# One core, linear-memory attention and MLP: first loads on two queues, segment 0 in token halves, its blocks in borrowed space, a new order of work

## The chip, the cores and the metric

One core of a Trainium2 chip runs the kernel. The metric is device time in microseconds. The kernel before has a median of 305.55 us over three runs (305.26 to 305.59). The profile and its trace are of one separate execution, whose span from the first to the last instruction is 303.6 us.

## The reference

One pre-norm transformer block over 2048 tokens of width 640: attention with 32 heads of 20, in 4 segments of 512 tokens with a running memory, and then an MLP of width 1728.

```python
h  = x + A(layernorm(x))          # A: attention below, wq wk wv wo of 640x640
h2 = h + silu(layernorm(h) @ w1) @ w2

# A, for each segment s of 512 tokens, M and z start at 0
p     = softmax(q_s k_s^T * 20**-0.5 + causal mask)
a_dot = p @ v_s
a_mem = (phi(q_s) @ M) / (phi(q_s) @ z + 1e-6)
o_s   = sigmoid(beta) * a_mem + (1 - sigmoid(beta)) * a_dot
M, z  = M + phi(k_s)^T v_s, z + sum(phi(k_s))
# phi(t) = t + 1 where t > 0, else exp(t); the output is o @ wo
```

Inputs, weights and output are bf16; sums are kept in f32.

## The kernel before, in words

The program is a list of some 1,500 small tasks written out by hand in `ORDER` (L358 to L457). `Graph.schedule` (L287) reads it: each entry names a task, its engine where it has a choice (`/A` ACT, `/D` DVE, `/G` POOL) and the buffer slots it takes. Each engine gets its own tasks in the order of the list and works them off in that order. `Tracker.add` (L79) finds out which earlier task wrote or still reads what a task touches, and puts a wait in front of it. A waiting task holds up everything behind it on its engine. DMA starts are instructions of such a queue too: nearly all stand on SP, two on ACT.

The steps of a segment s (of four blocks of 128 tokens) and their names:

- `x0` to `x3`, `x4`, `x8`, `x12` load x (`load_x`, L564): one block each for the first four, four blocks at a time for the others. `w_wv`, `w_q`, `w_k` load the attention weights; wq and wk land in the space of `sT` and are copied into groups of four heads by `re_wq0` to `re_wk4` (L663).
- `n1_stB`, `n1_raB`, `n1_rbB`, `n1_apB` are the layer norm of block B (L701): statistics on DVE, variance + eps and the power -0.5 on POOL, then the scaling on DVE. For blocks 0 to 3 PE transposes the result (`n1_tpB`) and ACT or DVE copies it out of PSUM (`n1_teB`); the later ones are transposed by a DMA (`n1_trB`).
- `vSI` and `veSI` are the V projection of a block and its way out of PSUM (L783, L794). `prSCW` projects head group C, for Q (W = 0) or K (W = 1), over all 512 tokens in five matmuls (L817), and `qeSCW` casts it to bf16 (L826 on DVE, L825 on ACT). PSUM has eight banks of 512 f32 columns, and the list says which one a task takes.
- Heads have 20 rows of 32, so the remaining 12 rows hold parts of heads 20 to 31; 12 small DMAs per segment (`vt`, L857) put these together in `QKV`, for the head groups (ticks) 5 to 7.
- A tick is one group of four heads: `qk` scores in four row tiles (L893), `e` exponentials on ACT (L904), `mk` causal masks on POOL (L915), `av` the product with V in four column tiles (L936), `oe` out of PSUM, `tn` back to token order, `nm` the division. In segment 0 each tick is worked in two halves of the tokens: `x` for the first 256 and `y` for the last.
- `ex`, `pha`, `phb` make phi; `kt`, `mz`, `ma`, `mb` the memory; `ot`, `wo`, `rs` the output projection and the residual; `n2_` the second layer norm, transposed into `hT`; `h1`, `th`, `s` the first MLP product and its activation (L1153, L1162, L1168); `h2`, `o`, `out` the second product, the residual and the store (L1195, L1208, L1213). The last 64 of the 1728 hidden columns (`h1_S_13`) are done in two column tiles of 64 (L1148).
- `fillN` are N matmuls on zeros (L604) that compute nothing.

In segment 0 `wq`, `wk` and `wv` come in the order wv, wq, wk, behind x1 and x0 on SP, with x3 and x2 on ACT. `w1` is loaded in five pieces and `w2` in six, at various places of SP's queue.

Of the kernel before, what the change touches and what calls it, by code (L numbers as in the profile page):

```python
# [5 lines left out]
ACT = mybir.ActivationFunctionType  # L6
ALU = mybir.AluOpType
# [340 lines left out]
SPLIT0 = ()  # L348
# [10 lines left out]
zpad:0 vpad0 iota x3:4 x1:3 x0:7 x2:5 sel w_wv:0 warm:0 vpad1 w_q:0 w_k halfc epsc beta x4:0,1,2,6 n1_st0:1 w_wo:0  # L359
w_w2_4 n1_st1:6 n1_ra0 w_w1_0:0 n1_rb0 n1_ap0:0 n1_ra1 n1_st2:2 fill30:0 n1_tp0:4 n1_rb1 n1_te0/A:0 n1_st3:0 n1_ra2  # L360
epsg0 n1_rb2 fill8:1 v00:0 mt1 n1_ap2:1 n1_ra3 n1_ap1:0 n1_rb3 n1_tp1:2 n1_tp2:6 mt2 n1_ap3:2 n1_te1/A re_wq1/D:0
n1_tp3:4 n1_te2/A re_wq4/D v01:2 ve00/D:1 n1_te3/A re_wq2/A pr010:6 re_wk0/A:0 re_wk1/D ve01/D pr011:7 qe010/D:0
re_wk3/D re_wk4/A lsc0 lsc1 re_wq0/D pr001:0 re_wk2/D qe011/A qk1x0:4 qe001/D:0 pr000:1 e1x2:5 n1_st6:0 e1x0 pr021:0
re_wq3/D qe000/A n1_ra6 mk1x_0 lsc2 n1_st7:4 ex001:0 qk0x0:4 n1_rb6 pr020:2 e0x2:0 mt3 mk1x_256 qe021/D:0 e0x0 lsc3
pr041:3 n1_st5:5 qe020/A vt00:0 n1_st4:7 qk2x0:4 n1_ra5 qe041/A:0 mk0x_0 pr031:1 zf0 vt09 vt06 e2x2:2 n1_rb5 mk0x_256
pr030:0 e2x0 n1_ap5:2 pha041:1 x8:8,9,10,11 qe031/A:0 mk2x_0 vt03 qk0yb0:4 qe030/D av1x:3 e0yb0:1 pr040:2 mk2x_256
n1_ra7 pha001:0 e0yb2 oe1x/D:0 av0x:3 qe040/D mk0yb_0 qk1yb0:4 oe0x/A:1 av2x:0 e1yb0:3 tn1x:1 v03:2 pha021:2 nm1x:3,0
e1yb2 mk0yb_256 phb001 n1_ap6:1 oe2x/A:0 mk1yb_0 qk3x0:4 ve03/D v02:0 n1_tr5:0 vt011 vt07 e3x2:4 vt04 n1_rb7 n1_st9:1
e3x0 ex021:2 ve02/D vt05 vt010 qk4x0:4 mk3x_0 n1_ra4 tn0x:2 e4x0:6 nm0x:0 vt01 mk3x_256 e4x2 n1_st8:6 fill7:3 qk0ya0:0
mta1 vt02 av3x:4 e0ya0:5 mk4x_0 vt08 oe3x/D:1 n1_st10:0 mk4x_256 e0ya2 fill6:5 qk1ya0:4 n1_tr6 v11:0 n1_rb4 e1ya0:0  # L370
n1_st11:3 n1_ra10 mta3 kt00:1 n1_ra8 e1ya2 av4x:2 ve11/D:0 tn2x:3 n1_ra11 phb021 qk5x0:4 n1_ap4:3 fill10:0 v12:0 e5x2:2
n1_ap7:1 n1_tr4 oe4x/D:0 e5x0 nm2x:1 ex011:2 n1_tr7 ve12/D qk6x0:4 mk5x_0 tn4x:2 e6x0:4 av0y:3 nm4x:0 mk5x_256 tn3x:0
e6x2 oe0y/D:0 kt02:0 n1_rb11 av5x:1 ex041:1 n1_ap11:3 qk7x0:4 mk6x_0 v10:2 nm3x:1 w_w2_5 e7x2:6 oe5x/D:1 mta2 mtb3 e7x0
mk6x_256 w_w1_1 w_w1_4 ve10/D qk2ya0:4 mk7x_0 v13:0 e2ya2:5 n1_ra9 mk7x_256 mk1yb_256 e2ya0 tn0y:2 av7x:3 ve13/D n1_rb8
oe7x/A:0 qk2yb0:4 nm0y:1 tn7x:0 e2yb0:1 av6x:1 nm7x:2 tn5x:2 av1y:3 e2yb2 oe6x/D:1 nm5x:3 tn6x:0 oe1y/A:0 qk3ya0:4
# [24 lines left out]
mk12e_0 qk13b0:4 qe231/D:0 tn11:2 e13b2:5 pr200:0 mk12e_256 nm11:3,0 ad10 e13b0 av12:1 qe200/D:0 mk13b_0 qk14a0:4 v23:2  # L400
e14a2:1 phb140 mk13b_384 oe12/D:1 mb04:0 e14a0 av13:1 ve23/A qk14b0:4 mz13:0 e14b2:3 pr221:2 ma13 oe13/D:0 e14b0
h1_0_7_1:3 qe221/A mk14b_0 qk14e0:4 th0_7_1:1 tn13:0 s0_7_1 mk14a_0 pr211:2 nm13:3,1 mk14b_384 e14e0:0 e14e2 h1_0_8_1:3
qe211/D mk14e_0 qk15a0:4 th0_8_1:1 pr241:0 e15a0:4 s0_8_1 mk14e_256 ad11 e15a2 av14:2 qe241/D:0 ad13 mz11:1 oe14/A:0
# [57 lines left out]
def build(nc, es, A_x, A_wq, A_wk, A_wv, A_wo, A_beta, B_x, B_w1, B_w2, out):  # L461
# [229 lines left out]
    for c in range(NC):  # L691
        load_w(f"w1_{c}", w1_sb[:, c, :], B_w1[128 * c:128 * c + 128, :], -1 + 0.2 * c, 1.4, [(W["w1"], [c])])
# [576 lines left out]
```

## Time and profile before

| | us |
|---|---|
| runs, median of 3 | 305.55 |
| span of the profiled execution | 303.6 |
| first filler on PE | 1.12 |
| first matmul of the computation (transposition of block 0) | 7.36 |
| first scores | 16.33 |
| first exponential | 16.72 |
| last matmuls begin | 289.81 (97 of L1195, 11.48) |

The costliest groups of instructions by engine:

| line | engine, what | count | busy us | mean ns |
|---|---|---|---|---|
| L904 | ACT, exponentials | 168 | 156.3 | 985 |
| L915 | POOL, masks | 128 | 81.5 | 650 |
| L1195 | PE, second MLP product | 462 | 64.8 | 295 |
| L1153 | PE, first MLP product | 325 | 62.5 | 337 |
| L1168 | DVE, activation | 70 | 37.6 | 558 |
| L604 | PE, fillers | 61 | 9.1 | 310 |

Busy time of PE counts each matmul from its start to its modelled end; dense matmuls start closer together than that. The fillers stand in it as busy. PEclk, the granted clock, is 1.00 in every window.

### The profile page before, as it was taken

The page shows a single profiled execution, that of the slowest core. Times are in us where ns is not written, and L with a number is a line of the kernel's source. Part 1 is how long each engine was busy: PE and PEld are TensorE (multiplying, and loading weights), DVE is VectorE, ACT ScalarE, POOL GpSimd, SP SyncE. Part 2 cuts the span into 40 slices and gives each one's busy share as a digit, 9 for nine tenths or more (in the row PEclk, how much of TensorE's full clock was granted, in tenths as well). Part 3 has the DMA queues.
Part 4 walks back from the last instruction along what each step waited for, and adds up shares of the span by engine and source line. Part 5 has one row for each costly group of instructions (what it writes and reads, how often), then busy time and mean ns, then how long its engine had stood idle before and what let it go on. Part 6 is the DMA issues. An engine that isn't in the chain of part 4 may idle for free.

```text
span 303.6 us, 7334 instructions
## 1 busy us (share of the span) xinstructions
PE 294.4 (97%) x2934; PEld 167.9 (55%) x2934; DVE 214.4 (71%) x492; ACT 226.6 (75%) x321; POOL 141.7 (47%) x280
## 2 busy tenths in 40 slices
PE   6999989999999999999999999999999999999996
PEld 5634545466565455566643545556564466764565
DVE  4888967877868866958588975858847494835623
ACT  3689988999999999899889989968779951004500
POOL 3346574532875856546847317564564730400000
PEclk9999999999999999999999999999999999999999
DMA  6938375843544130063551300043241006221003
GB/s 211 363 104 159 69 153 87 272 37 77 166 87 75 39 42 2 2 122 69 106 154 42 67 19 0 2 89 69 56 97 36 2 0 89 43 66 66 0 3 107
DMA packets 48721, 24.65 MB, mean 81 GB/s; under 512 B 39152, under 2 KB 47600, under 8 KB 48688
## 3 DMA queue, kind: packets, MB, share of 16 engines
q1 hardware_dynamic: 48400, 23.86, 34.6%
q8 instruction: 23, 0.38, 0.5%
q10 hardware_dynamic: 288, 0.33, 0.4%
q14 instruction: 10, 0.08, 0.1%
HBM read 10.41 MB, written 2.62 MB: 43 GB/s over the span
## 4 chain that ended last, share of the span: by engine, by line
PE 72%; ACT 12%; DVE 7%; DMA 4%; SPq 2%; issue 1%; POOL 0%; ACTq 0%
PE ps_all L1195 17%; PE ps_all L1153 13%; PE ps_all L817 13%; ACT PT L904 8%; PE ps_all L893 7%; PE ps_all L1119 6%; PE ps_all L783 5%; PE ps_all L936 5%; DVE sT L1168 3%; DMA wv_sb<-in_A_wv_dram 2%; ACT th L1162 2%; PE ps_all L965 2%; PE ps_all L1058 2%; DMA x_tok<-in_A_x_dram 1%; PE ps_all L969 1%
## 5 line engine op out<-in xcount | busy, mean ns | idle before, releaser
L904 ACT ACTIVATE PT<-ps_all 128x1024 bf16<-128x1024 f32 (+1 forms) x168 | 156.3, 985 | 16.9 <-PE ps_all L893 15.9
L915 POOL TENSOR_SCALAR_AFFINE_SELECT PT<-PT 128x512 bf16<-128x512 bf16 x128 | 81.5, 650 | 52.8 <-ACT PT L904 51.5
L1195 PE MATMUL ps_all<-w_sb,sT 128*128 128x320 bf16 (+2 forms) x462 | 64.8, 295 | 0.1
L1153 PE MATMUL ps_all<-hT,w_sb 128*128 128x512 bf16 (+1 forms) x325 | 62.5, 337 | 0.5 <-DVE sT L1168 0.4
L1162 ACT ACTIVATE th<-ps_all 128x512 f32<-128x512 f32 (+2 forms) x70 | 34.0, 505 | 35.1 <-PE ps_all L1153 24.6
L1168 DVE SCALAR_TENSOR_TENSOR sT<-th,ps_all 128x512 bf16<-128x512 f32 (+2 forms) x70 | 37.6, 558 | 23.8 <-ACT th L1162 23.2
L1195 PEld LDWEIGHTS ps_all<-w_sb,sT 128*128 128x128 bf16 x462 | 43.2, 98 | 18.5 <-issue 1.9
L1153 PEld LDWEIGHTS ps_all<-hT,w_sb 128*128 128x128 bf16 x325 | 29.8, 98 | 25.4 <-issue 2.1
L1010 POOL TENSOR_TENSOR otok<-on 128x320 bf16<-128x320 bf16 x24 | 19.2, 804 | 23.7 <-DVE on L1002 23.6
L711 DVE BATCH_NORM_STATS2 stt<-x_tok 128x6 f32<-128x320 bf16 x64 | 27.8, 476 | 3.4 <-DMA x_tok<-in_A_x_dram 3.2
L1208 DVE SCALAR_TENSOR_TENSOR x_tok<-ps_all,x_tok 128x640 bf16<-128x640 f32 (+3 forms) x18 | 13.3, 748 | 19.0 <-PE ps_all L1195 18.9
L720 POOL TENSOR_TENSOR rst<-mvt,eps_c 128x1 f32<-128x1 f32 x32 | 7.1, 223 | 40.4 <-DVE mvt L714 36.0
L817 PE MATMUL ps_all<-xT,wqr 128*128 128x512 bf16 x100 | 25.0, 381 | 0.0
L783 PE MATMUL ps_all<-wv_sb,xT 128*128 128x320 bf16 x160 | 24.4, 300 | 0.4 <-DMA wv_sb<-in_A_wv_dram 0.3
L817 PE MATMUL ps_all<-xT,wkr 128*128 128x512 bf16 x100 | 24.8, 380 | 0.0
L1119 PE MATMUL ps_all<-wo_sb,oT 128*128 128x320 bf16 x160 | 24.1, 299 | 0.4 <-DVE rd L996 0.2
L936 PE MATMUL ps_all<-PT,Vx 128*32 128x256 bf16 (+3 forms) x576 | 24.4, 287 | 0.0
L893 PE MATMUL ps_all<-QK 20*128 20x256 bf16 (+3 forms) x360 | 20.5, 286 | 1.0 <-ACT PT L904 0.7
L1002 DVE TENSOR_TENSOR on<-ps_all,rd 128x640 bf16<-128x640 f32 x24 | 19.8, 824 | 1.9 <-POOL otok L1010 1.1
L826 DVE CAST QK<-ps_all 128x512 bf16<-128x512 f32 x25 | 16.9, 684 | 5.1 <-PE ps_all L817 5.0
L1119 PEld LDWEIGHTS ps_all<-wo_sb,oT 128*128 128x128 bf16 x160 | 14.8, 97 | 8.1 <-issue 2.8
L783 PEld LDWEIGHTS ps_all<-wv_sb,xT 128*128 128x128 bf16 x160 | 14.7, 98 | 7.9 <-issue 1.5
(71 smaller groups left out, 329.4 us busy)
## 6 DMA issues: line engine op xcount, KB each, us to landing
out_dram<-x_tok SPq DMA_DIRECT2D x15, 160.0 KB, 1.9
w_sb<-in_B_w_dram SPq DMA_DIRECT2D x5, 432.0 KB, 4.5
x_tok<-in_A_x_dram SPq DMA_DIRECT2D x3, 640.0 KB, 5.3
w_sb<-in_B_w_dram SPq DMA_DIRECT2D x3, 480.0 KB, 3.8
QKV<-QK SPq DMA_DIRECT2D x16, 72.0 KB
wv_sb<-in_A_wv_dram SPq DMA_DIRECT2D x1, 800.0 KB, 7.2
sT<-in_A_wq_dram SPq DMA_DIRECT2D x1, 800.0 KB, 8.9
sT<-in_A_wk_dram SPq DMA_DIRECT2D x1, 800.0 KB, 10.6
```

Source lines behind the costliest of these rows:

```text
L711: T.add(DV, lambda e, hh=hh: e.bn_stats(out=stt[:, s, 6 * hh:6 * hh + 6], in_=xb[:, 320 * hh:320 * hh + 320]), reads=R((xa, xsub)), writes ...
L783: fns.append(lambda e, c=c, hh=hh: e.matmul(bank(ps, hh)[:, 0:320], lhsT=xT[:, c, 128 * i:128 * i + 128], rhs=wv_sb[:, c, 320 * hh:320 * h ...
L817: fns = [lambda e, kc=kc: e.matmul(bank(ps)[:, lo:hi], lhsT=wt[:, kc, c, :], rhs=xT[:, kc, lo:hi], start=(kc == 0), stop=(kc == NC - 1)) f ...
L893: fns.append(lambda e, j=j, o=o, r=r, q0=q0, q1=q1, qa=qa, ka=ka: e.matmul(ps_all[:, o:o + q1 - q0], lhsT=ka[32 * r:32 * r + DH, 128 * j:1 ...
L904: T.add(AC, lambda e: e.activation(out=pt[:, pta.slot, q0:q0 + 2, 0:width], in_=sc3[:, b0:b0 + 2, 0:width], func=ACT.Exp, scale=SCALE), re ...
L915: T.add(PO, lambda e: e.affine_select(out=v, in_=v, pattern=[[0, 4], [1, 128]], compare_op=ALU.is_ge, fill=0.0, base=0, channel_multiplier ...
L936: fns.append(lambda e, j=j, r=r, h=h, pa=pa, pt=pt, co=co, q0=q0, ji=ji: e.matmul(bank(po)[32 * r:32 * r + 32, q0:hi], lhsT=Vx[:, vx.slot, ...
L1119: fns.append(lambda e, c=c, hh=hh: e.matmul(bank(ps, hh)[:, 0:320], lhsT=oT[:, c, 128 * i:128 * i + 128], rhs=wo_sb[:, c, 320 * hh:320 * h ...
L1153: fns = [lambda e, c=c: e.matmul(bank(ps)[:, lo:hi], lhsT=w1_sb[:, c, 128 * f:128 * f + 128], rhs=hT[:, c, lo:hi], start=(c == 0), stop=(c ...
L1162: T.add(AC, lambda e: e.activation(out=th[:, tha.slot, lo:hi], in_=bank(ps)[:, lo:hi], func=ACT.Tanh, scale=0.5), reads=R((ps, [0])), writ ...
L1168: T.add(DV, lambda e: e.scalar_tensor_tensor(out=sT[:, f, lo:hi], in0=th[:, tha.slot, lo:hi], scalar=1.0, in1=bank(ps)[:, lo:hi], op0=ALU. ...
L1195: fns.append(lambda e, f=f, t0=t0, fr=fr, hh=hh, n=n: e.matmul(bank(pa, hh)[:, 0:n], lhsT=sT[:, f, t0:t0 + 128], rhs=w2_sb[:, fr, c0 + 320 ...
```

## The change

The first loads stand on both queues: SP has x0, wq, x2, the first three fifths of wv, beta, x4, wo, two small pieces of w2 and x8; ACT has x1, wk, its warm-up, x3, the rest of wv, and w1, now in one DMA.

```diff
-    load_x(1, 1, -99, 2.33, "fix", (SP,))
-    load_w("wv", wv_sb[:, :, :], cw(A_wv), -98, 4.96, [(W["wv"], [0])], "fix", (SP,))
-    load_x(2, 1, -97, 4.79, "fix", (AC,))
+    load_x(1, 1, -100, 2.33, "fix", (AC,))
+    load_w("q", wraw[:, 0, :, :], cw(A_wq), -99, 6.58, [(sT0, ["q"])], "fix", (SP,))
+    load_w("k", wraw[:, 1, :, :], cw(A_wk), -99, 8.51, [(sT0, ["k"])], "fix", (AC,))
+    load_x(2, 1, -97, 4.79, "fix", (SP,))
     load_x(3, 1, -96, 4.82, "fix", (AC,))
+    load_w("wv0", wv_sb[:, 0:3, :], cw(A_wv[0:384, :]), -95, 4.96, [(W["wv"], [0])], "fix", (SP,))
+    load_w("wv1", wv_sb[:, 3:5, :], cw(A_wv[384:640, :]), -95, 4.96, [(W["wv"], [1])], "fix", (AC,))
...
-    for c in range(NC):
-        load_w(f"w1_{c}", w1_sb[:, c, :], B_w1[128 * c:128 * c + 128, :], -1 + 0.2 * c, 1.4, [(W["w1"], [c])])
...
+    load_w("w1", w1_sb[:, :, :], cw(B_w1), -1, 7.0, [(W["w1"], range(5))], "plain", (AC,))
```

In segment 0 every Q and K projection is split into two of 256 tokens (`pr000x`, `pr000y` and so on). Its Q and K go into the space of `w2_sb` (`QZ`, `QZV`) and its transposed blocks into `hT`; four pieces of w2 are loaded once the scores of segment 0 have read that space.

```diff
-SPLIT0 = ()
+SPLIT0 = tuple((c, w) for c in range(5) for w in range(2))
...
+    QZ = w2_flat[:, 0:10 * L].rearrange("p (c w t) -> p c w t", c=5, w=2)
+    QZV = w2_flat[:, 10 * L:16 * L].rearrange("p (c w t) -> p c w t", c=3, w=2)
...
+    def load_w2():
+        qk, va = segs[0]["qk"], (segs[0]["qv"], list(range(12)))
+        WA = {0: [(qk[0], WH), (qk[1], WH), (qk[2], WH[:2])], 1: [(qk[2], WH[2:]), (qk[3], WH), (qk[4], WH[:2])],
+              2: [(qk[4], WH), va], 3: [va]}
...
-        xTa = G.alloc("xT")
+        xTa = G.alloc("xT" if s else "hT")
+        xT_ = xT if s else hT
```

`n1_ra` and `n1_rb` become one task `n1_r`, whose first step may run on DVE (its second stays on POOL). The scaling of the layer norm (`ap`), the first step of phi (`pha`) and the copies of wq and wk may run on POOL: 26 of 32 `ap`, 16 of 30 `pha` and `re_wq3` do. The last 64 hidden columns go into four column tiles of 32.

```diff
-                            bank(ps)[64 * k:64 * k + 64, lo:hi], lhsT=w1_sb[:, c, 128 * f:FF],
-                            rhs=hv[:, c, k, b0 // 2:b1 // 2, :], start=(c == 0), stop=(c == NC - 1),
-                            tile_position=(0, 64 * k)) for c in range(NC) for k in range(2)]
+                            bank(ps)[32 * k:32 * k + 32, lo:hi],
+                            lhsT=w1_sb[:, c, 128 * f + 32 * (k % 2):128 * f + 32 * (k % 2) + 32],
+                            rhs=hv[:, c, k // 2, b0 // 2:b1 // 2, :], start=(c == 0), stop=(c == NC - 1),
+                            tile_position=(0, 32 * k)) for c in range(NC) for k in range(4)]
```

The whole list is new. Its fillers are `fill54` and `fill9` instead of 30, 8, 7, 6 and 10. It ends with the middle 192 columns of the last block where the old one ended with its last 128. It begins:

```diff
+mt2:0 x0:7 w_q:0 x2:5 halfc mt1 mt0 mta1 mt3 iota mtb1 x1:3 mta0 epsc vpad0 mtb0 zpad mta2 mtb2 mm7 sel w_k mta3 epsg0
+mtb3 n1_st0:1 n1_r0/D w_wv0:0 beta n1_st1:6 n1_r1/D warm:0 x4:0,1,2,6 w_wo:0 w_w2_4 w_w2_5 n1_ap0/D:0 mm9 mm4 mm0
+n1_ap1/D:1 x3:4 w_wv1 x8:8,9,10,11 w_w1:0 re_wq0/D:0 re_wk0/D:0 mm1 mm10 n1_st2:2 re_wk1/D re_wq3/G mm8 mm5 re_wq1/D
+n1_r2/G n1_st3:0 n1_ap2/G:3 n1_r3/G mm11 mm6 mm3 re_wk2/D vpad1 fill54:0 n1_tp0:6 n1_te0/A:0 n1_tp1:3 n1_te1/A fill9:1
+mm2 re_wk3/D re_wq2/A pr000x:5 qe000x/A:0 pr001x:3 qe001x/A n1_ap3/D:2 pr030x:6 qe030x/A:0 qk0x0:0 e0x2:0 lsc0 zf0 zf1
+mzc1 mzc3 mzc8 mzc10 mzc2 lsc1 e0x0 mk0x_0 mzc7 mk0x_256 mzc0 pr010x:7 qe010x/D:0 n1_st11:2 re_wq4/D n1_st4:7 lsc2
+n1_r4/D n1_ap4/G:0 n1_tr4:0 mzc4 n1_st5:3 n1_r5/G lsc3 mzc11 n1_r11/D mzc9 n1_ap5/G:1 pr011x:6 n1_tp2:4 n1_te2/A mzc5
+pr021x:2 pr031x:3 mzc6 epsg1 qe021x/A:0 qe011x/A qe031x/A n1_tp3:0 n1_te3/A qk1x0:4 e1x2:1 pr020x:2 qe020x/A pr020y:0
+pr021y:3 pr011y:1 e1x0 mk1x_0 mk1x_256 qe011y/D pha011/G:0 qk2x0:4 qe021y/A qe020y/A pha021/D:2 re_wk4/A e2x2:2
+pr010y:2 qe010y/D pr000y:3 qe000y/D pr001y:0 qe001y/D vt03:0 vt06 vt00 vt09 pha001/D:1 e2x0 mk2x_0 n1_st10:0 n1_r10/D
+n1_st6:5 mk2x_256 n1_st9:1 n1_r9/D pr040y:1 qe040y/A:0 n1_st7:4 n1_r7/D ex011:0 phb011 ex001:1 phb001 n1_r6/D n1_st8:6
...
```

More of the change, by code (lines that the diff above doesn't have):

```diff
@@ L358 @@
 ORDER = """
[L359 to L363, printed above, removed]
@@ L796, in declare_front @@
             G.task(f"ve{s}{i}", {AC: act_c(640), DV: dve_c(640)}, e_ev, [(ps, [0])], [(vx, [i])], pr)
-        qk = [G.alloc(f"QK{c}") for c in range(5)]
+        QK_, QKV_ = (QZ, QZV) if s == 0 else (QK, QKV)
+        qk = [G.alloc(f"{'QK' if s else 'QZ'}{c}") for c in range(5)]
         pq = [G.alloc(f"pQ{c}") for c in range(5)] if s >= 1 else None
@@ L1131, in declare_back @@
         sa = G.alloc("sT")
-        parts = [(0, 2), (2, 4)] if s == 0 else [(0, 4)]
+        parts = [(0, 2), (2, 4)] if s == 0 and H1HALVES else [(0, 4)]
         for q, (b0, b1) in enumerate(parts):
@@ L1157, in declare_back @@
                 G.task(f"h1_{s}_{f}_{q}", {PE: pe_c(*[n] * 5) + (0.02 if tail else 0.0)}, e_mm,
-                       [(hTa, list(range(b0, b1))), (W["w1"], range(5))], [(ps, [0])], pr, mode="d" if tail else "f",
+                       [(hTa, list(range(b0, b1))), (W["w1"], range(5))], [(ps, [0])], pr, mode="c" if tail else "f",
                        reserve=[tha, sa])
```

254 lines of the change are left out of this document (129 added, 125 removed), and 1 row of the table pools.

## The prediction

> **What bounds it now.** I read the page's head and its table of slices first, then windows over the first 60 us, then timelines of the start, then the DMA issues, then the chain of waits.
>
> ```profile
> span 303.6 us, 7334 instructions
> PE 294.4 (97%) x2934; PEld 167.9 (55%) x2934; DVE 214.4 (71%) x492; ACT 226.6 (75%) x321; POOL 141.7 (47%) x280
> ...
> PE   6999989999999999999999999999999999999996
> ```
>
> PE is busy nearly everywhere, so only its work, its idle time and its fillers count. Windows (columns: length, busy time of PE, PEld, DVE, ACT, POOL with instruction counts, granted clock, DMA share, GB/s):
>
> ```profile
> 0.00:5.00 5.00, 3.88 (x21) 2.88 (x22) 1.10 (x3) 2.55 (x2) 1.70 (x11) 1.00 0.54 173
> 5.00:10.00 5.00, 3.45 (x32) 2.49 (x30) 4.86 (x15) 0.70 (x1) 3.08 (x10) 1.00 0.98 320
> 10.00:15.00 5.00, 4.93 (x40) 3.04 (x38) 3.69 (x12) 4.13 (x11) 0.60 (x2) 1.00 1.08 364
> ...
> 30.00:40.00 10.00, 9.17 (x131) 5.62 (x131) 8.47 (x25) 8.66 (x13) 5.99 (x14) 1.00 0.40 80
> 40.00:60.00 20.00, 18.83 (x235) 9.70 (x231) 15.58 (x45) 18.41 (x26) 11.20 (x25) 1.00 0.69 170
> ```
>
> DMA is full from 5 to 15 us. From 30 to 60 us ACT is nearly full and PE has holes. The timelines (start, duration, engine, line) and the issues give the sizes:
>
> ```profile
> 1.12 5.03 PE L604 MATMUL ps_all<-zpad 128*128 128x256 bf16 x30 [1.12 <-DVE zpad L583]
> 7.65 1.04 PE L604 MATMUL ps_all<-zpad 128*128 128x256 bf16 x8
> 9.03 1.52 PE L783 MATMUL ps_all<-wv_sb,xT 128*128 128x320 bf16 x10 [0.35 <-DMA wv_sb<-in_A_wv_dram]
> 16.33 0.34 PE L893 MATMUL ps_all<-QK 20*128 20x256 bf16 x8
> ...
> 6.77 1.92 SPq L570 DMA_DIRECT2D wo_sb<-in_A_wo_dram  x1
> ...
> wv_sb<-in_A_wv_dram SPq DMA_DIRECT2D x1, 800.0 KB, 7.2
> wo_sb<-in_A_wo_dram SPq DMA_DIRECT2D x1, 800.0 KB, 11.0
> ...
> 17.04 0.87 DVE L711 BATCH_NORM_STATS2 stt<-x_tok 128x6 f32<-128x320 bf16 x2
> 17.95 0.21 DVE L714 BATCH_NORM_AGGREGATE mvt<-stt 128x2 f32<-128x12 f32 x1
> ```
>
> **The accounting.** I write the span as PE work + PE lost + tail. Work is each matmul at its start-to-start time where they run densely (0.216 us for 512 columns, 0.136 for 320, 0.109 for 256, 0.056 for 128; row groups and column groups of four counted once), which sums to 261.0 us, plus 0.109 us for each change between full-array, row-tiled and column-tiled matmuls (a projection starts at 17.69, its five take 1.08, the scores behind start at 18.87). The old list has 222 such changes: 24.2 us. The tail behind the last matmul is 2.4. So 303.6 - 285.2 - 2.4 = 16.0 us are lost. Lost at a point is a task's start minus the work ahead of it: 8.8 us at the first V projection, 9.0 at 26.5 us, 13.1 at 40.6, 13.5 at 45, 14.0 at 65, 15.5 at 107, 16.1 at 290. More than half of the 7.3 us lost behind the start falls into 30 to 41 us, where ACT is the limit and 23 fillers stand in.
>
> **The change, the cheap parts.** The new list has 210 mode changes: 12 x 0.109 = -1.3 us. Halved projections: ten of 5 x 0.216 become twenty of 5 x 0.109, +0.1. The tail of the hidden layer in four column tiles: if four share the array as PV's do, 0; if only two, about 10 pairs x 0.105 more in each of five, of which two are halves, +2.4 at most; I take 0, since the PV row is the same form. The last store is 48 KB behind a 192-column add instead of 32 KB behind 128: +0.1. So work is 261.1 + 22.9 = 284.0, tail 2.5, and span = 286.5 + lost.
>
> POOL gets 26 normalisations and 16 of the max steps of phi. The trace has neither on POOL. The nearest rows: a mask of 512 elements 0.65 us, a two-input add of 320 elements 0.80; so 0.81 to 1.6 us for a normalisation, 0.65 to 1.3 for a phi. By the lower ends POOL rises from 123 to 159 us of dense time, about half the span: covered by PE unless its queue is held up. The last w2 piece is issued some 10 us of PE work ahead of its use, against 4.5 us to land: nothing, with 5 us of cover; without that cover it would cost what it is late.
>
> **The change, the start.** By the wo row, the 640 + 2400 + 8 + 640 + 800 = 4488 KB up to wo have landed at 6.77 + 11.0 = 17.8 us; by the wv row, the first 1440 KB at 8.9: 342 KB/us. Now x0, x1, wq, wk come first: 1920 KB at 8.9 + 480/342 = 10.3, say 10. Each filler takes 0.213 us until 4.3 us, then 0.109, so 54 end at 8.7; two transposes, ACT's copies (0.6 apart) and wq's rearrangement (0.45) bring the first half projection at 10.7, the first scores at 12.5 (16.33 before) and the second at 16.3, behind x2 and x3 (2240 KB, 11.2 us) and two of DVE's statistics (1.0 each). The work ahead of these second scores is 5.4 us: lost 11, against 8.8.
>
> **The step that decides** is one wait. DVE's new queue runs: statistics of blocks 2 and 3, rearrangements, the normalisation of block 3 (15.5), one Q eviction (16.2), and then the statistics of block **11**. Block 11 comes with x8, which the old kernel issued at 23.78 and used at 29.10. Now x8 is the last of ten loads on SP's queue, and w1, 2160 KB in one piece, stands on ACT's queue beside it. Up to x8 the chip must bring 640 + 1600 + 800 + 8 + 640 + 800 + 160 + 2160 + 640 = 7448 KB: 2960 KB past wo's mark, 8.7 us at 342, so **26.4 us**; at the best slice of the page (363 GB/s, 354 KB/us) 26.2, and with the start fuller by half a microsecond 25.5. If w1 got nothing until x8 is in, 5288 KB: 20.1 us. The two ends are 20.1 and 26.4. I take 25.5: in the first loads of before, two queues that both had work landed alike (3.1 us on ACT's, 3.3 on SP's), so neither went ahead.
>
> The Trainium skill, DMA: Bandwidth & Descriptors, Issuing engines are not separate DMA queues, says that transfers started by different engines share the same 16 DMA engines and interleave, and that a second issuer saves only issue time. By it w1 does take its part beside x8; the rows above agree.
>
> Behind that wait on DVE stand, in order: wq4's rearrangement (0.45), statistics of 4 and 5, four tiny ones, and then qe011y, the eviction that frees PSUM bank 1: 25.5 + 1.0 + 0.45 + 2.0 + 0.45 + 0.4 = 29.8. PE meanwhile runs on until 21.5 and stops at pr040y, which needs both wq4 and bank 1: 29.9 us, with 10.0 us of work ahead of it. **Lost: 19.9** instead of about 9.0. POOL waits too, on the 1/sigma of block 4, and holds the masks of tick 1; SP waits with the QKV copies on the four evictions behind qe011y. Next late is ACT: from pr040y's eviction to the last exponentials of e2yb it has 22.5 us of dense work, PE 21.0: +1.5, so 21.4. From there I take the old kernel's rise from 45 us on, 2.6: lost 24.0. Between none and twice these two items: 19.9 to 28.1.
>
> Sum: 286.5 + 24.0 = 310.5 us of span. The median of the runs, 305.55, stands 1.95 above the profiled span, so **312.5 us**, 2.3% slower. With 28.1 lost, x8 at 26.4 (+0.9) and 2.4 for the tiles, 320; with none of the two later items, 308.4.
>
> The Trainium skill, TensorE: Matmul & The Clock Gate, The HAM clock gate, says that an idle window of some 3.4 us halves TensorE's clock until it has been busy as long again. The first 30 fillers take 5.03 us and eight later ones 1.04, which agrees at the start, though the granted clock reads 1.00 there; no row shows it behind a hole in mid-kernel. By it PE would lose some 1.6 us more after 30 us, 314 in all.
>
> **Rivals.** (1) x8 arrives when DVE wants it, and the earlier scores pay: **faster**. For: ACT starts its exponentials four microseconds earlier, in the very stage it limits, and the fillers of 30 to 37 us are gone. Against: 7448 KB in 17 us. No stall, lost 11 + 1.5 + 2.6 = 15.1: 301.6 of span, 303.6 us. The two kernels are equal at 17.1 lost, 13.0 at pr040y, so with x8 at 18.6 us; below that it is faster. (2) SP's loads go well ahead of w1 and x8 lands near 20.1: pr040y at 24.5, lost 18.6, 307 us. For: w1 is issued only behind ACT's table load and warm-up (4.3 us) and wv1. Against: both queues have long been full by then. (3) POOL becomes the bound behind the stall: from the pow of block 4 to the masks of tick 7 it has 15.5 us by the lower prices, 18.5 by the higher, from 28 us on: 46.5, where PE would want tick 7 at 45.8; repeated in the next segments that is +4 and more: 317. Against: its share of the span stays near a half.
>
> **Numbers.** Forecast 0.62 (308 to 316), rival 1 0.15, rival 2 0.14, rival 3 0.09. The range reaches below into rivals 1 and 2 and above to 317: 304 to 317. 0.2% (0.6 us) is about what the runs can tell from no change: faster 0.15, within it 0.05 (the edge between rivals 1 and 2), slower 0.80.
>
> **What would show it.** Right: DVE idle for some 9 us before 25.5 us, ended by the DMA of x_tok; PE's slices at 22 to 30 us near 0, then projections of 256 columns; scores from 12.5 us; w1 landing before x8; PE's idle sum up by some 8 us, the rest as before. Wrong: x8 landing before 18.6 us, or PE passing pr040y by 23 us. The clock rule shows in the spacing of the matmuls right behind the hole.

## The result

| | us |
|---|---|
| forecast | 312.5 (304 to 317) |
| changed kernel, median of 4 runs | 363.25 (362.88 to 363.48) |
| kernel before, median of 4 runs beside them | 305.4 (305.19 to 305.59) |
| ratio, 95% interval | 1.189 (1.187 to 1.192) |
| span of the profiled execution after | 360.9 |

The sign was right and the size was not: 58 us slower, where 7 were forecast, and far outside the range. In the tables below, ratios go by the faster executions of a run and medians by all four; this matters for `all_dve`, which takes 350.1 us without its two slow ones.

**The profile after.** First the page (span, busy time by engine, then slices of 9 us in tenths):

```profile
span 360.9 us, 7562 instructions
...
PE 311.4 (86%) x3036; PEld 178.6 (49%) x3036; DVE 212.6 (59%) x476; ACT 224.0 (62%) x321; POOL 233.4 (65%) x306
...
POOL 6648996555759669885994896778499742370000
PEclk9998879999999699998969998999899999998999
```

No engine is full over the span. POOL has gained 92 us (141.7 before) and stands at 9 in several slices. The granted clock of TensorE, 1.00 in all windows of before, now has dips. The windows (columns as in the prediction) say where:

```profile
20.00:25.00 5.00, 4.29 (x51) 3.28 (x51) 0.00 (x0) 5.00 (x14) 1.91 (x7) 1.00 0.71 212
25.00:30.00 5.00, 0.91 (x8) 0.54 (x7) 4.85 (x20) 1.23 (x2) 2.06 (x2) 0.93 0.00 2
...
40.00:60.00 20.00, 14.26 (x180) 7.18 (x182) 13.73 (x39) 13.12 (x19) 19.73 (x25) 0.83 0.27 56
...
180.00:200.00 20.00, 19.99 (x189) 10.62 (x190) 8.16 (x15) 11.38 (x14) 14.22 (x15) 0.84 0.38 90
```

From 20 to 25 us DVE does nothing at all, and from 25 to 30 PE nearly nothing: the stall that was forecast. Its edges differ from the forecast: DVE comes to the wait at 19.6 us instead of 16.2, so it waits 5.4 us and not 9, and PE has work until 25.73 instead of 21.5. From 40 to 60 us POOL is busy for 19.73 of 20 us, PE for 14.26 instead of 18.83, and at a clock of 0.83. The timeline of the first 34 us (start, duration, engine, line; in brackets the idle time before and what ended it):

```profile
14.40 2.51 POOL L749 TENSOR_SCALAR xn_rot<-x_tok,mvt,rst 128x640 bf16<-128x640 bf16 x1
...
18.74 0.23 ACT L632 ACTIVATE bsel<-beta_bc 128x32 f32<-128x32 bf16 x1 [4.40 <-DMA beta_bc<-in_A_beta_dram]
...
25.04 0.89 DVE L727 BATCH_NORM_STATS2 stt<-x_tok 128x6 f32<-128x320 bf16 x2 [5.41 <-DMA x_tok<-in_A_x_dram]
...
25.02 0.71 PE L836 MATMUL ps_all<-hT,wkr 128*128 128x256 bf16 x5
29.82 1.25 PE L836 MATMUL ps_all<-hT,wqr 128*128 128x256 bf16 x5 [4.09 <-DVE w_sb L845]
...
33.22 0.72 PE L836 MATMUL ps_all<-hT,wkr 128*128 128x256 bf16 x5
```

x8 lands at 25.02 and ends DVE's wait; `pr040y` starts at 29.82 (forecast 25.5 and 29.9). The two lines above it are the start's own delays: the normalisation of block 2 on POOL takes 2.51 us, and ACT waits 4.40 us for beta. Five matmuls of 256 columns behind the hole take 1.25 us, later 0.72: half clock. In windows of 1 us (the granted clock is the third number from the right):

```profile
30.00:31.00 1.00, 1.00 (x6) 0.73 (x5) 0.96 (x4) 0.00 (x0) 1.00 (x1) 0.50 0.00 0
33.00:34.00 1.00, 1.00 (x17) 0.76 (x17) 0.96 (x4) 0.66 (x1) 1.00 (x1) 1.00 0.24 41
```

The view of groups (busy time, mean ns) shows the price that the prediction bounded without a row:

```profile
L749 POOL TENSOR_SCALAR xn_rot<-x_tok,mvt,rst 128x640 bf16<-128x640 bf16 x26 | 65.2, 2508 | 6.0 <-DMA hT<-xn_rot 4.4
L858 POOL TENSOR_SCALAR phiQ<-QK 128x512 bf16<-128x512 bf16 x10 | 19.2, 1921 | 0.0
```

2.51 and 1.92 us, where the prediction's ends were 0.81 to 1.6 and 0.65 to 1.3. The view of waits (total, times, longest) shows who pays for it:

```profile
PE ps_all L956 <- POOL PT L935: 16.4, 12, 3.4
...
DVE phiQ L864 <- POOL phiQ L858: 10.4, 5, 3.2
...
DVE phiK L864 <- POOL phiK L858: 7.0, 3, 3.1
```

In the kernel before, no matmul waits for a mask; the one wait of PE's there that ends at a mask stands at weight loads:

```profile
PEld ps_all L936 <- POOL PT L915: 2.1, 7, 0.4
```

In the changed kernel PV waits 16.4 us for masks (L935). One of these places in the timeline:

```profile
43.71 2.51 POOL L749 TENSOR_SCALAR xn_rot<-x_tok,mvt,rst 128x640 bf16<-128x640 bf16 x1
46.18 3.70 POOL L935 TENSOR_SCALAR_AFFINE_SELECT PT<-PT 128x512 bf16<-128x512 bf16 x6
...
48.75 0.35 PE L956 MATMUL ps_all<-PT,Vx 128*32 128x256 bf16 x8 [1.77 <-POOL PT L935]
```

A normalisation stands in POOL's queue ahead of six masks, and PE waits behind it.

**Time lost on PE**, in the terms of the prediction (start of a task minus the work ahead of it; work is 284.0 us in every version of the new list, 285.2 in the old):

| work ahead, us | 5 | 10 | 20 | 30 | 60 | 120 | 180 | 280 |
|---|---|---|---|---|---|---|---|---|
| before | 9.2 | 9.1 | 9.2 | 13.2 | 13.9 | 15.6 | 16.0 | 16.1 |
| after | 14.9 | 20.3 | 25.2 | 30.8 | 36.2 | 51.1 | 64.3 | 74.3 |
| after, short steps on POOL (`cheap_pool`) | 14.2 | 19.9 | 21.5 | 23.9 | 24.6 | 27.0 | 28.7 | 28.6 |
| the same without the wait for x8 (`cheap_late`) | 9.9 | 12.4 | 16.5 | 18.7 | 19.5 | 22.0 | 23.7 | 23.6 |

Up to 10 us of work the forecast (19.9) holds. Behind it the changed kernel loses another 54 us, a little everywhere up to the last segment. The last two rows belong to runs of the next section.

### The profile page after: what moved, and what is told of

It reads as the page before. It is cut to its first block, busy times and chain, and to the rows that moved or that the text cites. A ratio compares the mean times of both kernels' runs of the same rounds, so it can differ in the third digit from the quotient of the medians.

```text
span 360.9 us, 7562 instructions
## 1 busy us (share of the span) xinstructions
PE 311.4 (86%) x3036; PEld 178.6 (49%) x3036; DVE 212.6 (59%) x476; ACT 224.0 (62%) x321; POOL 233.4 (65%) x306
## 4 chain that ended last, share of the span: by engine, by line
PE 40%; POOL 30%; DMA 11%; DVE 10%; ACT 5%; issue 3%; SPq 1%; POOLq 1%; ACTq 0%
POOL xn_rot L749 11%; PE ps_all L1174 10%; PE ps_all L1216 9%; POOL PT L935 8%; DMA x_tok<-in_A_x_dram 4%; PE ps_all L1139 4%; PE ps_all L956 4%; POOL phiQ L858 4%; PE ps_all L836 4%; ACT PT L924 3%; DMA hT<-xn_rot 3%; PE ps_all L801 3%; POOL rst L743 3%; PE ps_all L913 3%; DMA sT<-in_A_wq_dram 3%
## 5 line engine op out<-in xcount | busy, mean ns | idle before, releaser
L935 POOL TENSOR_SCALAR_AFFINE_SELECT PT<-PT 128x512 bf16<-128x512 bf16 x128 | 81.3, 647 | 33.9 <-ACT PT L924 31.5
L749 POOL TENSOR_SCALAR xn_rot<-x_tok,mvt,rst 128x640 bf16<-128x640 bf16 x26 | 65.2, 2508 | 6.0 <-DMA hT<-xn_rot 4.4
L1216 PE MATMUL ps_all<-w_sb,sT 128*128 128x320 bf16 (+2 forms) x462 | 67.2, 303 | 0.0
L1189 DVE SCALAR_TENSOR_TENSOR sT<-th,ps_all 128x512 bf16<-128x512 f32 (+2 forms) x70 | 37.6, 558 | 25.2 <-ACT th L1183 24.6
L956 PE MATMUL ps_all<-PT,Vx 128*32 128x256 bf16 (+3 forms) x576 | 26.7, 310 | 19.1 <-POOL PT L935 16.4
L743 POOL TENSOR_TENSOR rst<-rst,eps_c 128x1 f32<-128x1 f32 x32 | 18.3, 576 | 21.8 <-DVE rst L737 20.8
L956 PEld LDWEIGHTS ps_all<-PT,Vx 128*32 128x32 bf16 x576 | 13.1, 100 | 31.3 <-POOL PT L935 12.5
L1139 PE MATMUL ps_all<-wo_sb,oT 128*128 128x320 bf16 x160 | 26.4, 320 | 0.3 <-DVE rd L1016 0.3
L971 DVE TENSOR_SCALAR oTs<-ps_all,lsc 128x512 bf16<-128x512 f32 (+1 forms) x31 | 19.5, 633 | 11.9 <-PE ps_all L956 11.7
L801 PE MATMUL ps_all<-wv_sb,xT 128*128 128x320 bf16 x120 | 20.4, 322 | 4.0 <-DVE sT L1189 2.0
L836 PE MATMUL ps_all<-xT,wkr 128*128 128x512 bf16 x75 | 18.8, 381 | 1.3 <-DVE oTs L971 1.3
L858 POOL TENSOR_SCALAR phiQ<-QK 128x512 bf16<-128x512 bf16 x10 | 19.2, 1921 | 0.0
```

The lines of the kernel that those rows point to most:

```text
L749: T.add(eng, lambda e: e.tensor_scalar(out=xn_rot[:, xn.slot, :], in0=x_tok[:, b % 12, :], scalar1=mvt[:, s, 0:1], scalar2=rst[:, s, :], o ...
L801: fns.append(lambda e, c=c, hh=hh: e.matmul(bank(ps, hh)[:, 0:320], lhsT=xT_[:, c, 128 * i:128 * i + 128], rhs=wv_sb[:, c, 320 * hh:320 * ...
L836: fns = [lambda e, kc=kc: e.matmul(bank(ps)[:, lo:hi], lhsT=wt[:, kc, c, :], rhs=xT_[:, kc, lo:hi], start=(kc == 0), stop=(kc == NC - 1)) ...
L858: T.add(eng, lambda e: e.tensor_scalar(out=o, in0=QK_[:, c, w, :], scalar1=0.0, scalar2=1.0, op0=ALU.max, op1=ALU.add), reads=R((qk[c], wa ...
L935: T.add(PO, lambda e: e.affine_select(out=v, in_=v, pattern=[[0, 4], [1, 128]], compare_op=ALU.is_ge, fill=0.0, base=0, channel_multiplier ...
L956: fns.append(lambda e, j=j, r=r, h=h, pa=pa, pt=pt, co=co, q0=q0, ji=ji: e.matmul(bank(po)[32 * r:32 * r + 32, q0:hi], lhsT=Vx[:, vx.slot, ...
```

## The experiments

Each kernel ran beside the kernel before on the same chip. The expectations name theories by letters: **P**, the price of the 42 steps moved to POOL; **S** and **C**, the hole at 25 to 30 us and the half clock behind holes; **L** and **M**, the new list has other waits; and, for the runs with the steps on DVE, **T**, the time that they add there, **D**, DVE's waits for the power -0.5 that stays on POOL, and **O**, the order of the steps in DVE's queue.

### The price on POOL

The first try at it was the obvious one, the 42 steps back on DVE (below); it did not isolate the price. These do.

`cheap_pool` leaves list and engines alone and shortens the steps to 208 of 640 and 172 of 512 columns; the rest of the columns is left out:

```diff
-            T.add(eng, lambda e: e.tensor_scalar(out=xn_rot[:, xn.slot, :], in0=x_tok[:, b % 12, :],
+            n = 208 if eng == PO else D
+            T.add(eng, lambda e: e.tensor_scalar(out=xn_rot[:, xn.slot, 0:n], in0=x_tok[:, b % 12, 0:n],
...
-                        o = phiQ[:, c, :] if w == 0 else phiK[:, pa.slot, :]
+                        n = 172 if eng == PO else L
+                        o = phiQ[:, c, 0:n] if w == 0 else phiK[:, pa.slot, 0:n]
```

> The changed kernel with its list and engines untouched, but the 26 normalisations on POOL do only the first 208 of 640 columns and the 16 phi steps on POOL only the first 172 of 512; the other columns are set to zero once at the start, so the output is another one. At 2.51 and 1.92 us for the whole that makes 0.82 and 0.65 us each, the lower ends that the prediction took. Theory P (POOL's price alone is what the sum lacked): POOL's busy time falls from 233 by 26 x 1.69 + 16 x 1.27 = 64 to about 169 us, the time falls to 310 to 318 us, and the granted clock goes up with it. Theory M (the list has a second set of waits between DVE, the transposing DMAs and SP's rows of small issues, which the prediction did not price, and which kept the run with all of it on DVE at 353 us): 335 to 350 us.

**317.9 us**, ratio 1.042 (1.039 to 1.045). The steps took 1.07 and 0.80 us, not 0.82 and 0.65, so this is a price inside the prediction's two ends:

```profile
L753 POOL TENSOR_SCALAR xn_rot<-x_tok,mvt,rst 128x208 bf16<-128x208 bf16 x26 | 28.0, 1078 | 5.0 <-DMA hT<-xn_rot 3.4
L863 POOL TENSOR_SCALAR phiQ<-QK 128x172 bf16<-128x172 bf16 x10 | 8.1, 810 | 0.0
```

POOL's busy time fell by 54 us and the time by 45. The same stretch of time as above:

```profile
40.00:60.00 20.00, 17.93 (x242) 10.03 (x230) 14.73 (x38) 17.55 (x25) 12.50 (x20) 1.00 0.52 105
```

POOL has air, PE is back at 17.93 and the clock at 1.00. Its waits on masks:

```profile
PE ps_all L961 <- POOL PT L940: 1.9, 5, 0.5
```

1.9 us instead of 16.4. The time lies at the upper edge of what theory P gave (310 to 318) and far from what M gave (335 to 350), so P holds for the changed kernel.

`before_ap_pool` and `before_ap_short` put the same 26 normalisations on POOL in the kernel before, whole and on 208 columns:

```diff
-            T.add(DV, lambda e: e.tensor_scalar(out=xn_rot[:, xn.slot, :], in0=x_tok[:, b % 12, :],
+            T.add(eng, lambda e: e.tensor_scalar(out=xn_rot[:, xn.slot, :], in0=x_tok[:, b % 12, :],
...
-pr030:0 e2x0 n1_ap5:2 pha041:1
+pr030:0 e2x0 n1_ap5/G:2 pha041:1
```

> The kernel before, its list unchanged, with the same 26 normalisations put on POOL and nothing else. Theory P: POOL's busy time rises from 142 by 65 to 207 us and its queue, not its total, decides: masks stand behind normalisations of 2.51 us, three or four of them in a row at each segment's start: 320 to 345 us, the granted clock below 1. If the price on POOL hurts only behind the hole at 22 to 30 us (rival C) or only in the new list (rival L): 305 to 312 us.

> The kernel before with the 26 normalisations on POOL (349 us), on 208 of 640 columns: 1.07 instead of 2.51 us each, POOL's busy time 37 us lower, near 169. If the price is what cost it the 43 us, it falls to 305 to 312 us; if it is the place in POOL's queue, whatever the step takes, above 330 us.

**348.7 us** (ratio 1.144, 1.140 to 1.149) and **313.0 us** (1.026, 1.024 to 1.028). So the old list, with no late x8 at all, loses 43 us to the price of 26 of these steps; shortened, 8 are left. Both times lie above what was expected, 348.7 by 4 us (320 to 345) and 313.0 by 1 (305 to 312). The 8 us that are left also say that steps of some 1.1 us, inside the prediction's ends, are not covered by PE. The waits of the whole and of the short one:

```profile
PE ps_all L936 <- POOL PT L915: 16.3, 10, 4.0
```

```profile
PE ps_all L939 <- POOL PT L918: 6.0, 5, 2.4
```

`price` measures forms of instruction at the end of POOL's queue, where it is idle:

```diff
+    rows = [
+        lambda e: e.tensor_scalar(out=scr[:, :], in0=src, scalar1=mvt[:, 0, 0:1], scalar2=rst[:, 0, :],
+                                  op0=ALU.subtract, op1=ALU.mult),
...
+        lambda e: e.tensor_copy(out=scr[:, :], in_=src),
+    ]
+    for fn in rows:
+        for _ in range(2):
+            T.add(PO, fn, reads=R((W["wv"], [0])), writes=[("scr", 0, 0)])
```

> The kernel before with twelve more instructions at the end of POOL's queue, each form twice on 128 x 640 bf16: the normalisation (two operations, scalars from memory), max and add (two operations, constants), max alone, mult alone, a two-input add, a copy. From 2.51 us for 640 columns and 1.07 for 208 the normalisation costs 3.3 ns a column. If that is the price of two operations one after the other, the single ones take about 1.3 us; if it is the price of the instruction, they take 2.4 us too. The add by the row of 320 columns at 0.80: 1.6 us.

The answer by source line (name, count, then shortest, median and longest ns):

```profile
L1234 POOL TENSOR_SCALAR scr<-wv_sb,mvt,rst x2: 2496/2505/2514, 264.9 to 267.5; 128x640 bf16<-128x640 bf16 x2
L1236 POOL TENSOR_SCALAR scr<-wv_sb x2: 2347/2354/2362, 270.1 to 272.6; 128x640 bf16<-128x640 bf16 x2
L1237 POOL TENSOR_SCALAR scr<-wv_sb x2: 1807/1810/1812, 275.0 to 276.9; 128x640 bf16<-128x640 bf16 x2
L1238 POOL TENSOR_SCALAR scr<-wv_sb,mvt x2: 1880/1882/1885, 278.8 to 280.8; 128x640 bf16<-128x640 bf16 x2
L1239 POOL TENSOR_TENSOR scr<-wv_sb x2: 1393/1397/1401, 282.8 to 284.2; 128x640 bf16<-128x640 bf16 x2
L1240 POOL COPY scr<-wv_sb x2: 717/720/722, 285.7 to 286.5; 128x640 bf16<-128x640 bf16 x2
```

Neither guess was right. One scalar operation costs 1.81 to 1.88 us, a second 0.54 to 0.62 more; the two-input add (1.40) is cheaper than either, and the copy takes 0.72. The rows that bounded the price in the prediction, a mask and an add, are other forms.

### The wait for x8

`st_late` moves the statistics of blocks 8 to 11 back in the list, behind work of 30 to 45 us, so that DVE meets x8 when it has landed; `cheap_late` does it in `cheap_pool`. `cheap_late_beta` also issues beta earlier on SP (it stood fifth there and comes third, not from sixth to second as the expectation counts). `tiny_late` is `cheap_late` with 16 columns in each step.

```diff
-mzc1 mzc3 mzc8 mzc10 mzc2 lsc1 e0x0 mk0x_0 mzc7 mk0x_256 mzc0 pr010x:7 qe010x/D:0 n1_st11:2 re_wq4/D n1_st4:7 lsc2
-n1_r4/D n1_ap4/G:0 n1_tr4:0 mzc4 n1_st5:3 n1_r5/G lsc3 mzc11 n1_r11/D mzc9 n1_ap5/G:1 pr011x:6 n1_tp2:4 n1_te2/A mzc5
+mzc1 mzc3 mzc8 mzc10 mzc2 lsc1 e0x0 mk0x_0 mzc7 mk0x_256 mzc0 pr010x:7 qe010x/D:0 re_wq4/D n1_st4:7 lsc2
+n1_r4/D n1_ap4/G:0 n1_tr4:0 mzc4 n1_st5:3 n1_r5/G lsc3 mzc11 mzc9 n1_ap5/G:1 pr011x:6 n1_tp2:4 n1_te2/A mzc5
...
-vt08 n1_tr5 phb021 kt02:1
+vt08 n1_tr5 phb021 n1_st11:2 n1_r11/D kt02:1
```

and, for beta:

```diff
-x0:7 w_q:0 x2:5
+x0:7 w_q:0 beta x2:5
```

> The changed kernel with the statistics of blocks 8 to 11 (and what follows them directly) moved back in the list, behind the work of 30 to 45 us, so that DVE does not wait for x8 at 16 to 25 us; loads and engines untouched. The wait of 5.4 us at the statistics is gone. Theory P: POOL is full from 28 us on, so most of the gain is given back: 354 to 363 us. Theory S (the hole of 22 to 30 us is what makes everything behind it late, by the clock and by backlogs): 315 to 335 us, granted clock above 0.98.

> Both together: the POOL steps on 208 and 172 columns, and the statistics of blocks 8 to 11 moved back. Theory P: no stall and POOL at the price that the prediction took, so what the first rival of the prediction gave, plus the late start of the second scores: 303 to 310 us. Theory M: 325 to 345 us.

> As the one before, and the small load of beta, 8 KB, stands second on SP instead of sixth, so that ACT does not wait for it until 18.7 us. The second scores start near 17 us instead of 19 to 21: 2 to 3 us less than the run before by theory P; no difference where another wait ends last (theory M).

> As the run with the POOL steps on 208 and 172 columns and the statistics of blocks 8 to 11 moved back (313 us), but with 16 columns each. What the price of 1.07 and 0.80 us still costs goes away: if that is the whole distance to the kernel before, 305 to 308 us; if the new list has its own losses at the start, 310 to 313 us.

| | us | ratio (95%) |
|---|---|---|
| `st_late` | 356.2 | 1.167 (1.162 to 1.173) |
| `cheap_late` | 313.0 | 1.026 (1.023 to 1.029) |
| `cheap_late_beta` | 313.9 | 1.028 (1.024 to 1.033) |
| `tiny_late` | 309.9 | 1.016 (1.014 to 1.017) |

Without the stall the changed kernel is 7.1 us faster and the one with short steps 5.0, so theory S falls: the hole does not make the rest. `cheap_late` stands 3 us above the range that theory P gave. With the stall gone and the 42 steps at 0.44 and 0.28 us (`tiny_late`, just below its 310 to 313), the new list is still 4.9 us slower than the kernel before; from `cheap_late` to `tiny_late`, steps inside the prediction's ends cost 3.1 us.

The 7.1 and 5.0 us hold more than the moved statistics. In the profiled executions of `st_late`, `cheap_late` and `tiny_late`, wq landed at 7.5 to 7.6 us and beta at 12.5 to 13.4; in the changed kernel and `cheap_pool` it was 10.5 and 9.9 us for wq, 18.7 and 18.0 for beta, with the same loads issued in the same order and, up to beta, at nearly the same times. What makes them land otherwise was not found. In `cheap_late` ACT therefore waits 0.22 us for beta (4.40 in the changed kernel), and the second scores start at 15.66 us (21.08). How much of the gain is this start is not shown. For the same reason `cheap_late_beta` (beta at 12.01) says only that an earlier beta brings nothing where ACT hardly waits for it; what it would bring in the changed kernel was not run. And DVE without the stall comes to x4 next, which lands at 19.34 us in `cheap_late`, and waits 3.26 us for it.

### The half clock

`after_fill` puts 259 fillers (L614) in front of 21 tasks of the changed kernel before which PE was idle for 1.1 us or more:

```diff
-mk2x_256 n1_st9:1 n1_r9/D pr040y:1
+mk2x_256 n1_st9:1 n1_r9/D fill27:1 pr040y:1
...
-kt24:1 th1_8_0:1 av21:6
+kt24:1 th1_8_0:1 fill23:7 av21:6
```

> The changed kernel with 259 more fillers (28 us of PE at full clock) in front of 21 tasks before which its profile shows PE idle for 1.1 us or more, each group as long as 0.7 of the hole it stands in; nothing else. The mean granted clock of the changed kernel is 0.948, so that 0.052 x 361 = 19 us of full-speed work are at most lost to it. Theory C (the half clock behind holes is a good part of the loss): the clock comes to 0.98 or more and the time falls to 345 to 357 us. Theory P alone (PE only waits for POOL, and a slower PE hides in the next wait): 360 to 366 us.

**352.6 us**, ratio 1.159 (1.153 to 1.164), clock 0.990 instead of 0.948. More work on PE, and 10.7 us less time. In the changed kernel's profile the granted clock is 0.50 in nine stretches of 3.41 or 6.83 us, 37.5 us together; in that of `after_fill` in one, of 6.83 us. Its window:

```profile
40.00:60.00 20.00, 17.80 (x236) 10.53 (x237) 12.91 (x37) 16.93 (x26) 19.41 (x24) 1.00 0.47 62
```

POOL is as full as in after (19.41). Of PE's 17.80 us, 2.63 are fillers, and the matmuls that compute are 215 instead of 180 in the same 20 us, at a clock of 1.00 instead of 0.83. So of the 58 us that the change costs, some 11 are matmuls at half speed behind stretches in which PE had too little to do. How many of the 11 belong to the price of the steps is not shown: one of the 21 places is the stall for x8, and two lie before it.

### The steps on DVE

```diff
-n1_r4/D n1_ap4/G:0 n1_tr4:0 mzc4
+n1_r4/D n1_ap4/D:0 n1_tr4:0 mzc4
...
-phb140 pha110/G:0 mk7yb_256
+phb140 pha110/D:0 mk7yb_256
```

In `dve_defer`, and then in `dve_far`, for instance:

```diff
-x12 s1_4_0 n1_st12:0 n1_r12/D n1_ap12/D:1 n1_tr12:0 ad16 n1_st15:1 n1_r15/G
+x12 s1_4_0 n1_st12:0 n1_r12/D ad16 n1_st15:1 n1_r15/G n1_ap12/D:1 n1_tr12:0
...
-phb140 pha110/D:0 mk7yb_256
+phb140 mk7yb_256
...
-vt11 vt14 phb110 vt17
+vt11 vt14 vt17
...
-h2_0_3 o0 out0
+h2_0_3 o0 pha110/D:0 phb110 out0
```

The short ones cut the steps to 208 and 172 columns as above.

> The changed kernel with all 26 normalisations and all 16 phi steps that it has on POOL put on DVE, at the same places of the list; everything else, the wait for x8 included, stays. Theory P (POOL's price: 2.51 us for a normalisation, 1.92 for a phi step, so that the masks behind them come late): POOL's busy time falls from 233 by 26 x 2.51 + 16 x 1.92 = 96 to about 137 us, DVE's rises by 26 x 0.45 + 16 x 0.29 = 16 us, the stop at pr040y stays near 29.8 us, and nothing like it follows: 310 to 318 us, the sum of the prediction. Rival C (the hole at 22 to 30 us starts it: behind it the granted clock stays below 1 and PE cannot catch up): the time stays above 340 us with the granted clock still near 0.95. Rival L (the new list itself, with its order of scores, PV and projections): also above 340 us, but at a granted clock near 1.

> The changed kernel with the 26 normalisations alone on DVE, the 16 phi steps stay on POOL. Theory P: POOL's busy time falls by 65 us to 168; most of the loss goes with it: 315 to 330 us. Rivals C and L: above 340 us.

> The changed kernel with the 16 phi steps alone on DVE, the 26 normalisations stay on POOL. Theory P: POOL's busy time falls by 31 us to 202, and the 40 to 60 us stretch, where POOL is full with normalisations and masks, hardly changes: 340 to 355 us. Rivals C and L: no change, 358 to 364 us.

> As the run with all 26 normalisations and 16 phi steps on DVE (353 us), but with 18 of the normalisations, and the transposing DMAs behind them, moved back in the list by up to three tasks of DVE, so that DVE has other work while POOL raises the variance to the power -0.5. Theory D (that run lost its gain because DVE, in order, waited 16.1 us in 19 places for that power): the waits at L743 fall below 4 us and the time to 312 to 325 us. If it stays above 340 us, the waits on the power were not what held it.

> The same, and the statistics of blocks 8 to 11 moved back as well. Theory D with the stall at x8 gone: 305 to 318 us, 5 us below the run before, as it was with the cheaper POOL steps. Otherwise above 335 us.

> The run with all 42 steps on DVE (353 us), but those 42 do only 208 and 172 columns there too; list unchanged, other columns zero. Theory T (it is DVE's added time, 26 x 0.45 + 16 x 0.29 = 16 us at the places where the list has DVE full): the time falls to 325 us or less. Theory O (it is the order: DVE stands in line for the power of POOL at 19 places, whatever the step then takes): above 340 us, with the waits at the power still near 16 us.

> All 42 steps on DVE, statistics of blocks 8 to 11 moved back, and now the normalisations up to six tasks of DVE later than they stood (three in the run before), and the first steps of phi directly before their second ones, up to two tasks later. Theory O (the list has nothing between the power and the scaling, or between the transposition that frees a phi buffer and the step that refills it, because it has POOL in mind; DVE, in order, waits there and all its evictions behind it): DVE's waits at the scalings and at phi fall from 17 to below 8 us and the time below 330 us. If the waits fall and the time stays near 338 us, the cause is another one, and stays open.

> The run before (all 42 steps on DVE, moved back as far as tried, 338 us) with the 42 steps also shortened to 208 and 172 columns, the other columns zero. If DVE's added time and its waits in line together are the whole matter, this comes to the 313 us of the run with short steps on POOL, at most 320. If it stays above 328 us, the places of the 42 steps in DVE's queue cost even when they are short and late, and where that arises stays open.

| run | us | ratio (95%) |
|---|---|---|
| `all_dve`: all 42 on DVE | 353.2 | 1.148 (1.139 to 1.156) |
| `ap_dve`: normalisations only | 355.7 | 1.170 (1.162 to 1.179) |
| `phi_dve`: phi steps only | 355.1 | 1.162 (1.155 to 1.168) |
| `short_dve`: all, 208 and 172 columns | 345.6 | 1.131 (1.125 to 1.136) |
| `dve_defer`: all, up to three tasks later | 344.8 | 1.131 (1.126 to 1.135) |
| `dve_defer_late`: and no wait for x8 | 337.6 | 1.107 (1.099 to 1.115) |
| `dve_far`: and up to six tasks later | 338.4 | 1.104 (1.097 to 1.111) |
| `short_far`: `dve_far`, 208 and 172 columns | 333.3 | 1.094 (1.087 to 1.100) |

Theory P had put the first at 310 to 318 and the second at 315 to 330. Both missed, and came where the rivals C and L had put them (above 340); `phi_dve` came at the upper end of its 340 to 355. What speaks for P are `cheap_pool` and `before_ap_pool`, not these runs. POOL's busy time did fall to 140 us, but a new wait came in its place (waits of `all_dve`):

```profile
DVE xn_rot L749 <- POOL rst L743: 16.1, 19, 2.1
```

The list has the scaling right behind the power -0.5, which stays on POOL; on DVE the scaling waits for it and holds up the evictions behind it. In the kernel before the same wait is 3.4 us. Theory D named it; moving the scalings back by three tasks brought it to 6.9 us, but the time to 344.8, not to 312 to 325. `short_dve`, with the waits still at 15.9 us, came where theory O had it. `dve_far` did not reach the condition of its expectation, waits below 8 us at these steps: 11.4 were left at the scalings, 6.7 for the power and 4.7 for the transposing DMA that frees their buffer. Shorter and later together (`short_far`) leave 333, 20 us above the same steps, equally short, on POOL (313). DVE waits 11.3 us at its scalings there, 6.6 for the power and 4.7 for the DMA; in `cheap_late` DVE waits 2.1 us for the power, and the 3.4 us for the DMA stand on POOL. One such wait of `short_far` can be followed to PE: DVE stands for the DMA until 62.49 us, the cast of Q behind it ends at 62.74, ACT has waited 5.33 us for it, and PE's next scores start at 64.84, after a hole of 4.48 us. So these waits are a part of the 20 us; how large a part, and what the rest is, stays **open**.

## Why the prediction was wrong

By its own steps:

- **Work, mode changes, four column tiles, tail**: right. The twenty matmuls of `h1_1_13` start within 0.458 us, the ten of before within 0.464: the 0 that was taken, not 2.4. With 74.3 lost, 284.0 of work and a tail of 2.6 the span is 360.9.
- **The start**: first projection 11.40 (forecast 10.7), first scores 13.13 (12.5), second 21.08 (16.3), so 15.6 lost there instead of 11. Two terms were missing: the normalisation of block 2 on POOL was priced at nothing (PE stood 1.7 us for it), and beta, 8 KB, fifth on SP, landed at 18.72 while ACT stood waiting for it with the exponentials behind (PE stood 1.4 us for these). The premise that neither queue goes ahead of the other did not hold: ACT's queue had landed 3600 KB by 18.54 us, SP's 1608 KB by 18.72, so the 2160 KB of w1 went ahead of the 8 KB of beta. In `cheap_late`, where SP's loads landed first, the second scores start at 15.66, earlier than forecast.
- **The wait for x8**: right in place, in order and in time, 19.9 lost at `pr040y`. It lands behind w1 (18.54), as the sum over both queues had it: 7448 KB are in at 25.02 us, where 25.5 was forecast. That SP issued it only at 15.12 us is not what made it late: in `cheap_late` it was issued at 11.04 and landed at 24.99. What failed is its worth, 5 to 7 us instead of the 9 of rival 1 (303.6 without it, where `cheap_late` has 313). One reason is that x4 lands only 4.7 us ahead of x8 (20.34), and DVE without the stall waits for x4. In `cheap_late` `pr040y` starts at 22.39 with 12.4 us lost, about rival 1's own schedule; the 23.6 lost in the end are 8.5 more than rival 1's 15.1, and 7 of these come behind `pr040y`.
- **POOL**: the step that failed. "So 0.81 to 1.6 us for a normalisation, 0.65 to 1.3 for a phi ... covered by PE unless its queue is held up." The price was 2.51 and 1.92, above both upper ends: 26 x 2.51 + 16 x 1.92 = 96 us on POOL instead of 32. At 1.07 and 0.80 the kernel takes 317.9, 5.4 above the forecast; the rest, **45 of the 51 us missed**, is this term, a part of it by way of the half clock. "Covered" failed too. It was argued from POOL's share of the span, and 65% still looks covered. It was not: 19.73 of 20 us between 40 and 60, with masks behind the steps and PV behind the masks; and even short steps left 8 us in `before_ap_short`.
- **Later rise**: 4.1 was forecast behind `pr040y`, with short steps it was 8.7 (19.9 to 28.6). That is 4.6 of the 5.4; its cause was not looked for beyond the 3.1 us from `cheap_late` to `tiny_late`.
- **Rival 3**, POOL as the bound (0.09, 317 us), was the right mechanism with the price at the same too low ends and only one recurrence counted. **Rivals 1 and 2** fell with x8 at 25.02.
- **The clock rule** was weighed and given 1.6 us for one hole. At that hole this is about right: the granted clock is 0.50 from 29.28 to 32.69 us, with 256-column matmuls 0.21 us apart, then 0.11; PE worked 2.87 us of it, which at half speed is some 1.4 us lost, by this estimate. The Trainium skill, TensorE: Matmul & The Clock Gate, The HAM clock gate, puts the time to come back at about 3.4 us; the trace agrees, 3.41. But the changed kernel pays again in eight more stretches, and `after_fill` got 10.7 us back. An idle window of 3.4 us is too narrow a condition for them: in the 3.41 us ahead of seven of them PE was busy for 1.0 to 1.8 us.

The direction of the price was in the prediction; its size was not to be had from a row of the trace. The Trainium skill, GPSIMD Engine Reference, Engine selection, advises elementwise work on VectorE and puts GPSIMD at about half its speed for two inputs, one input at roughly line rate. The trace of before has 0.45 us on DVE (median of 32; mean 0.52), that of after 2.51 on POOL, for one and the same normalisation with one input tensor: a factor of 5.6, so here the measurement decides against the milder figure. Taking the nearest rows (a mask, an add) for a form that the trace had only on DVE was the choice that failed; the range ended at 317 us, where these ends had put rival 3, and no other row held it there.

No run beat the kernel before, and none points to one that would: even with almost free steps on POOL and no stall, the new list stays at 309.9.

## What to carry to other kernels

An operation that the trace has on one engine has no price on another: before a list is rearranged around it, measure that very form there, or leave its upper end open. A share of the span does not say that an engine is covered; look for the stretch where its queue is full, and at what stands behind the long instruction in it. And undo a step by shrinking it in place, since moving it back can change the order for everything on the other engine as well.

## What was not expected of the hardware

- On POOL a step with scalars costs 0.38 us and 3.3 ns a column (normalisation: 0.44 us for 16 columns, 1.07 for 208, 2.51 for 640), always the same whatever ran beside it (2499 to 2532 ns in 26 cases). A two-input add of 640 columns is faster (1.40 us) than max alone (1.81).
- Issuing a transfer can take long: on SP the issue of wo took 4.00 us and that of two pieces of 80 KB 6.83 us, with large loads on both queues under way; the issue of x0 took 0.41. Here it decided nothing, since x8 landed at 25.0 us whether it was issued at 15.1 or at 11.0.
- The same loads, issued in the same order, landed at other times from one kernel to the other: beta at 18.72 us in the changed kernel, at 12.5 to 13.4 in `st_late`, `cheap_late` and `tiny_late`.
- The clock fell to half also behind stretches of 3.41 us in which PE was busy for 1.0 to 1.8 us.
- Matmuls that compute nothing made a kernel faster by 10.7 us, though PE was busy for 86% of its span without them.
